# Attention and two expert layers on one core: element steps ahead of low parts, and the opening and operand steps in another order

## The chip, the cores and the metric

The kernel runs on one core of a Trainium2 chip. The metric is the device time in microseconds of the whole program. Engines: PE is TensorE, DVE is VectorE, ACT is ScalarE, POOL is GpSimd, SP is SyncE, which issues the DMAs.

## The reference, cut to what matters

```python
def sm_attn(qq, kk, vv):
    s = scale * np.matmul(qq, kk.transpose(0, 1, 3, 2))
    s = s - np.max(s, axis=-1, keepdims=True)
    a = np.exp(s)
    a = a / (np.sum(a, axis=-1, keepdims=True) + 1e-09)
    return np.matmul(a, vv)
p_packed = sm_attn(p, k, v)                 # 32 packed rows per head
x = sm_attn(q, p_packed, p_packed)          # 8 batches, 8 heads, 576 tokens, 64 wide

xn = x / sqrt(mean(x * x) + 1e-06) * rms_g  # x as 4608 tokens x 512
g = xn @ w_gate                             # 512 x 1536
y = (g * (1.0 / (1.0 + np.exp(-g))) * (xn @ w_val)) @ w_out

h = y @ w_in                                # 512 x 2048
out = (np.maximum(h, 0.0) + alpha * np.minimum(h, 0.0)) @ w_out2
```

All inputs and outputs are float32.

## The kernel before

**Precision.** A product that must be exact to float32 is made of three matmuls in a rounded type (`mm3`, L122 to L124): high by high, high by low, low by high. For each operand ScalarE writes the high part (`split_hi`, L110) and VectorE then subtracts it from the source to give the low part (`split_lo`, L113). In the names h is the high part and l the low one: hh and hl of the activated tile s, in_h and in_l of the output weights, xh and xl of the normed tokens, yh and yl of an operand of the second layer.

**Attention in chains.** `k_steps` makes the packed rows of a batch, `q_steps` (L574 to L697) the tokens of a pair of tiles from them: transposes of q, a product, max (L628), subtraction (L630), Exp on ScalarE, sum and reciprocal (L636 to L638), multiplication (L640), transposition to A2T (L645), a product on TensorE (L656), squares on ScalarE (L680), the factor of the RMS norm (L683, L684 on VectorE, then a power step on GpSimd, L687), its transposition on TensorE (L692) and A2T times factor (L696). A chain stops at each yield; its kind says what may come next: E an element step on VectorE, X one on ScalarE, M and R others, a number a step that needs PSUM banks.

**First layer.** The 4608 tokens go in 12 chunks (0 to 11) of 512 or 320 tokens. In a chunk a loop over 12 slices f of the hidden width does: gate product (`blk_in`), activation s, value product, s times value (L1071), `hsplit` of s into hh and hl, and one slice late the output product (`blk_out(f - 1)`). Between these stand `work(f, at)`, which advances the attention chains of the next chunk (at is the place in the slice, 1 to 4), and `burst`, which issues their TensorE parts; `both` splits the output weights of the next slice. In chunk 0 the even slices use unsplit float32, so only odd slices have low parts.

**Opening.** The gate, value and output weights come as 64-bit words and are narrowed in units, by `narrow`: a first step (L227 on VectorE, L231 on ScalarE) and a second one (L233 on VectorE, L236 on GpSimd). `conv(2)` advances a pair of units by one step. Units 0 to 3 are gv_raw, 4 and 5 are w_raw, then gv_raw again. `wg_job(0, 0)` (L724 and following) multiplies units 0 to 3 by the packed rows of batch 0 in two halves (L733), the first from units 0 and 1, the second from 2 and 3. The lines of the opening from L789 on interleave by hand the chains qa and qb (first and second tile pair of chunk 0) and `conv`. Loads of later units wait until the slots of narrowed ones are free.

**Second layer.** Five pairs of token blocks (twice 512, three times, and twice 384 twice) are multiplied by a scheme of seven products. `prep` (L848 and following) makes the seven operands of a pair, for two halves kk, from y that the first layer stored: differences on VectorE (`less`, L861) and splits. `load_rows(pair, kk)` (L836 to L843) loads y on SP. `prep(0)` runs through the last chunk, `prep(pr + 1)` in the part of pair pr that computes 41 output blocks of the table LATER, in the order b5, c2, b6, d3, a1 (8 blocks each, and one c4): one step at each odd index k_, the rest at the pair's end. Ahead of a c2 block (n == 2) `combine_next` adds a subtraction (L1144) on VectorE.

The order of the instructions on each engine is that of the code: the schedule is manual.

Of the kernel before, what the change touches and what calls it, by code (L numbers as in the profile page):

```python
# [18 lines left out]
def attention_moe_moe2_kernel(ctx, tc, q, k, v, p, w_gate, w_val, w_out, rms_g, w_in2, w_out2, alpha, out):  # L19
# [8 lines left out]
    NF = FF // 128  # L28
# [32 lines left out]
    NP1 = len(CH)  # L61
# [50 lines left out]
    def split_lo(lo, src, hi):  # L112
        nc.vector.tensor_tensor(out=lo, in0=src, in1=hi.bitcast(F32), op=ALU.subtract)  # L113
# [12 lines left out]
    with tc.manual_schedule():  # L126
# [227 lines left out]
        steady, KEPT = [0], 1  # L354
        have, NRO = set(), {"h": 2, "l": 3}

        def both(u):
            h, l = [ring.tile([128, 4, 128], F32R, tag="o" + x, name="in_" + x, bufs=NRO[x]) for x in "hl"]
            split_hi(h, raw[u])
            lf, kept = l.rearrange("p c x -> p (c x)").bitcast(F32), lo_dram[u[1]]  # L360
            if u[1] in have and steady[0] > KEPT:
                nc.sync.dma_start(out=lf, in_=kept)
            elif steady[0]:
                nc.gpsimd.tensor_tensor(out=l, in0=raw[u], in1=h.bitcast(F32), op=ALU.subtract)
            else:
                split_lo(l, raw[u], h)
            if steady[0] == KEPT:
                nc.sync.dma_start(out=kept, in_=lf)
                have.add(u[1])
            in_s[u] = (h, l)  # L370
# [430 lines left out]
        xh, xl = new_x()  # L801
# [6 lines left out]
        some(qb, 6)  # L808
        conv(2)
        warmup(3)  # L810
        some(qa, 4)
        some(qb, 3)
        conv(2)
        warmup(3)
        some(qa, 3)
        x_split(ids_a, xh, xl, o_a)
        some(qb, 4)
        conv(2)
        conv_to(4)
        wg_job(0, 0)  # L820
        some(qb, 3)
        x_split(ids_b, xh, xl, o_b)
        assert qa.kind is None and qb.kind is None
        conv_to(5)

        def hsplit(h, n):
            hh = ring.tile([128, T], F32R, tag="hh", name="hh")[:, 0:n]
            hl = ring.tile([128, T], F32R, tag="hl", name="hl")[:, 0:n]
            split_hi(hh, h)
            split_lo(hl, h, hh)  # L830
            return hh, hl

        OPERANDS = ("b11", "b21", "b22", "t4", "t1", "t2", "t3")
# [97 lines left out]
        for c, (t0, n, cuts) in enumerate(CH):  # L931
# [106 lines left out]
            for f in range(NF):  # L1038
                if c == 0 and f == 1:
                    held, hold[0] = hold[0], None  # L1040
                    for i in held:
                        load_q(i)
                if c == 6 and f == 6:
                    nc.sync.dma_start(out=alpha_sb, in_=alpha.rearrange("(f p) -> p f", p=128))
                if c == 0:
# [2 lines left out]
                if last:  # L1048
                    if f == 0:
                        assert next(late, late) is late  # L1050
                        y_rows.append(load_rows(0, 0))
                        prepare = prep(0)
                    if f > 0:
                        next(prepare, None)
                    if f in (2, 4, 6, 8, 10):
                        next(prepare, None)
                    if f > 2:
                        load_next()
# [12 lines left out]
                nc.vector.tensor_tensor(out=s, in0=s, in1=tv, op=ALU.mult)  # L1071
                for jb in JOBS[c].get(f, ()) if c else ():
                    wg_job(*jb)
                hs[f] = s if c == 0 and f % 2 == 0 else hsplit(s, n)
                work(f, 2)
                burst(f, 2)
                work(f, 3)
                late_step(c, f, True)
# [119 lines left out]
        for pr, (t0, w) in enumerate(PAIRS):  # L1198
# [148 lines left out]
            for k_ in range(2, len(LATER)):  # L1347
                combine_next(k_ + 2)
                if k_ + 1 < len(LATER):
                    next(splits[k_ + 1])  # L1350
                next(splits[k_])
                while len(fill) > LAG:
                    fill.pop(0)()
                if after:
                    one_after()
                elif k_ % 2:
                    next(prepare, None)
            for _ in prepare:
                pass
# [37 lines left out]
```

## Time and profile before

| | |
|---|---|
| runs, us | 1611.49, 1612.0, 1614.06 (median 1612.0) |
| profiled execution, us | 1614.24 |
| its span, first to last instruction, us | 1612.5 |
| TensorE busy | 1564.3 us, 97% of the span |
| VectorE busy | 1156.4 us, 72% |
| ScalarE busy | 886.8 us, 55% |
| GpSimd busy | 174.6 us, 11% |
| mean granted clock of TensorE | 0.988 |

Some 1.7 us of the profiled execution lie outside the span. The stages in its time: opening to 52 us, chunk 0 to 162, chunks 1 to 10 to 845, chunk 11 to 889, then the second layer. Busy time of TensorE includes time in which a matmul of a group waits for the next operand inside it, so short waits are best read from the start times of neighbouring instructions and the "idle before" in brackets, which names what ended the wait.

### The profile page before, as it was taken

The page shows a single profiled execution, that of the slowest core. Times are in us where ns is not written, and L with a number is a line of the kernel's source. Part 1 is how long each engine was busy: PE and PEld are TensorE (multiplying, and loading weights), DVE is VectorE, ACT ScalarE, POOL GpSimd, SP SyncE. Part 2 cuts the span into 40 slices and gives each one's busy share as a digit, 9 for nine tenths or more (in the row PEclk, how much of TensorE's full clock was granted, in tenths as well). Part 3 has the DMA queues.
Part 4 walks back from the last instruction along what each step waited for, and adds up shares of the span by engine and source line. Part 5 has one row for each costly group of instructions (what it writes and reads, how often), then busy time and mean ns, then how long its engine had stood idle before and what let it go on. Part 6 is the DMA issues. An engine that isn't in the chain of part 4 may idle for free.

```text
span 1612.5 us, 31856 instructions
## 1 busy us (share of the span) xinstructions
PE 1564.3 (97%) x11762; PEld 1369.4 (85%) x11762; DVE 1156.4 (72%) x2232; ACT 886.8 (55%) x1894; POOL 174.6 (11%) x178
## 2 busy tenths in 40 slices
PE   7699999999999999999999999999999999999999
PEld 5366887887888988888888889988998899999998
DVE  4776666666666766767666678867877797788785
ACT  4556555555456555655555555554654464565554
POOL 1542230111201111112120000000000000000000
PEclk8799999999999999999999999999999999999999
DMA  9886777756777565785646676767676767788876
GB/s 244 255 262 201 232 237 226 244 163 209 246 234 231 163 226 188 251 265 164 209 145 210 185 213 191 242 203 217 182 248 202 211 188 244 261 263 284 263 244 196
DMA packets 239067, 356.29 MB, mean 221 GB/s; under 512 B 63424, under 2 KB 97216, under 8 KB 238912
## 3 DMA queue, kind: packets, MB, share of 16 engines
q1 hardware_dynamic: 238912, 354.25, 70.5%
q8 instruction: 94, 1.54, 0.4%
q14 instruction: 61, 0.50, 0.1%
HBM read 296.50 MB, written 57.67 MB: 220 GB/s over the span
## 4 chain that ended last, share of the span: by engine, by line
PE 80%; DVE 10%; ACT 5%; DMA 3%; issue 1%; SPq 1%; POOL 0%; DVEq 0%; ACTq 0%
PE ps_g L122 12%; PE ps_g L123 12%; PE ps_g L124 12%; PE ps_y L122 9%; PE ps_y L124 8%; PE ps_y L123 8%; PE ps_wg L733 3%; PE ps_v L122 2%; PE ps_v L123 2%; PE ps_v L124 2%; DVE hl L113 2%; PE ps_y L1031 1%; ACT hh L110 1%; DVE wgl L113 1%; DVE s L1071 1%
## 5 line engine op out<-in xcount | busy, mean ns | idle before, releaser
L122 PE MATMUL ps_g<-yh,w 128*128 128x512 f32 (+1 forms) x560 | 206.4, 369 | 0.0
L123 PE MATMUL ps_g<-yl,w 128*128 128x512 f32 (+1 forms) x560 | 206.3, 368 | 0.0
L124 PE MATMUL ps_g<-yh,w 128*128 128x512 f32 (+1 forms) x560 | 205.7, 367 | 0.0
L122 PE MATMUL ps_y<-hh,in_h 128*128 128x320 f32 (+1 forms) x552 | 195.1, 353 | 2.7 <-ACT hh L110 2.6
L123 PE MATMUL ps_y<-hl,in_h 128*128 128x320 f32 (+1 forms) x552 | 185.5, 336 | 2.3 <-DVE hl L113 2.1
L124 PE MATMUL ps_y<-hh,in_l 128*128 128x320 f32 (+1 forms) x552 | 184.4, 334 | 0.0
L110 ACT ACTIVATE hh<-kept 128x512 fp32r<-128x512 f32 (+1 forms) x200 | 116.4, 587 | 102.2 <-PE ps_g L123 49.2
L124 PE MATMUL ps_y<-w,hl 128*128 128x256 f32 x576 | 164.7, 286 | 3.1 <-DVE hl L113 2.3
L123 PE MATMUL ps_y<-w,hh 128*128 128x256 f32 x576 | 162.7, 283 | 0.0
L122 PE MATMUL ps_y<-w,hh 128*128 128x256 f32 x576 | 162.5, 282 | 0.0
L110 ACT ACTIVATE hh<-s 128x320 fp32r<-128x320 f32 (+1 forms) x138 | 71.9, 521 | 149.8 <-DVE s L1071 149.6
L122 PEld LDWEIGHTS ps_y<-hh,in_h 128*128 128x128 f32 x552 | 103.6, 188 | 49.9 <-issue 38.3
L113 DVE TENSOR_TENSOR hl<-kept,hh 128x512 fp32r<-128x512 f32 (+1 forms) x200 | 123.2, 631 | 16.0 <-ACT hh L110 14.9
L1141 DVE TENSOR_TENSOR tmp<-tmp,ps_g 128x512 f32<-128x512 f32 (+2 forms) x140 | 88.3, 631 | 56.0 <-PE ps_g L124 55.9
L124 PE MATMUL ps_g<-w,hl 128*128 128x256 f32 x432 | 122.4, 283 | 0.0
L122 PE MATMUL ps_g<-w,hh 128*128 128x256 f32 x432 | 122.3, 283 | 0.0
L123 PE MATMUL ps_g<-w,hh 128*128 128x256 f32 x432 | 122.3, 283 | 0.0
L113 DVE TENSOR_TENSOR hl<-s,hh 128x320 fp32r<-128x320 f32 (+1 forms) x138 | 77.8, 564 | 56.7 <-ACT hh L110 56.7
L122 PE MATMUL ps_g<-xh,wgh 128*128 128x256 f32 (+3 forms) x352 | 114.2, 324 | 3.3 <-ACT qT L600 1.8
L124 PEld LDWEIGHTS ps_g<-yh,w 128*128 128x128 f32 x560 | 105.2, 188 | 13.4
L122 PEld LDWEIGHTS ps_g<-yh,w 128*128 128x128 f32 x560 | 105.4, 188 | 11.9
L124 PEld LDWEIGHTS ps_y<-w,hl 128*128 128x128 f32 x576 | 109.9, 191 | 6.3 <-DVE hl L113 5.7
(199 smaller groups left out, 4068.9 us busy)
## 6 DMA issues: line engine op xcount, KB each, us to landing
w<-w_dram SPq DMA_DIRECT2D x280, 256.0 KB, 3.1
w<-o_dram SPq DMA_DIRECT2D x280, 256.0 KB, 3.0
gv_raw<-gv_dram SPq DMA_DIRECT2D x168, 256.0 KB, 4.1
in_l<-lo_dram SPq DMA_DIRECT2D x119, 256.0 KB, 4.5
w<-in_moe_w_out_dram SPq DMA_DIRECT2D x28, 512.0 KB, 5.2
w_dram<-w7o SPq DMA_DIRECT2D x56, 256.0 KB, 2.5
o_dram<-w7o SPq DMA_DIRECT2D x56, 256.0 KB, 2.9
vt<-in_v_dram SPq DMA_DIRECT2D x16, 576.0 KB, 6.2
```

The source lines that it names most:

```text
L110: nc.scalar.activation(out=hi, in_=src, func=ACTF.Copy)
L113: nc.vector.tensor_tensor(out=lo, in0=src, in1=hi.bitcast(F32), op=ALU.subtract)
L122: nc.tensor.matmul(out=o, lhsT=lh, rhs=rh, start=first, stop=False, skip_group_check=more)
L123: nc.tensor.matmul(out=o, lhsT=lh, rhs=rl, start=False, stop=False, skip_group_check=more)
L124: nc.tensor.matmul(out=o, lhsT=ll, rhs=rh, start=False, stop=last, skip_group_check=more)
L733: nc.tensor.matmul(out=ts[g][h * NP:(h + 1) * NP, :], lhsT=ppG[b][e * D:(e + 1) * D, c_, :], rhs=us[c_][e * D:(e + 1) * D, :], start=True, ...
L1031: nc.tensor.matmul(out=ybk[d], lhsT=w[:, d, :], rhs=h, start=f == 0, stop=f == NF - 1)
L1071: nc.vector.tensor_tensor(out=s, in0=s, in1=tv, op=ALU.mult)
L1141: nc.vector.tensor_tensor(out=out, in0=x, in1=y, op=ALU.add)
```

## The change

It moves instructions; their number and kinds stay the same, and TensorE's order too. (A) In the opening the second narrowing step of units 2 and 3 comes ahead of the second tile pair's factor. (B) In chunk 0 the low part of the output weights waits for the next `hsplit`. (C) In chunks 1 to 10, at slices 1 to 9, the chains' steps of place 2 come between hh and hl. (D) The first y rows are loaded in slice 9 of chunk 10 instead of slice 0 of chunk 11. (E) No operand step is issued at an odd index with a c2 block among the next three.

```diff
--- before.py
+++ after.py
@@ -354,6 +354,8 @@
         steady, KEPT = [0], 1
         have, NRO = set(), {"h": 2, "l": 3}
 
+        lo_later = []
+
         def both(u):
             h, l = [ring.tile([128, 4, 128], F32R, tag="o" + x, name="in_" + x, bufs=NRO[x]) for x in "hl"]
             split_hi(h, raw[u])
@@ -363,7 +365,7 @@
             elif steady[0]:
                 nc.gpsimd.tensor_tensor(out=l, in0=raw[u], in1=h.bitcast(F32), op=ALU.subtract)
             else:
-                split_lo(l, raw[u], h)
+                lo_later.append(lambda: split_lo(l, raw[u], h))
             if steady[0] == KEPT:
                 nc.sync.dma_start(out=kept, in_=lf)
                 have.add(u[1])
@@ -808,18 +810,21 @@
         some(qb, 6)
         conv(2)
         warmup(3)
-        some(qa, 4)
+        some(qa, 3)
+        conv(2)
+        some(qa, 1)
+        warmup(3)
+        some(qb, 3)
+        some(qa, 3)
+        conv(2)
+        x_split(ids_a, xh, xl, o_a)
         some(qb, 3)
         conv(2)
-        warmup(3)
-        some(qa, 3)
-        x_split(ids_a, xh, xl, o_a)
-        some(qb, 4)
-        conv(2)
-        conv_to(4)
+        some(qb, 1)
         wg_job(0, 0)
         some(qb, 3)
         x_split(ids_b, xh, xl, o_b)
+        conv(2)
         assert qa.kind is None and qb.kind is None
         conv_to(5)
 
@@ -827,7 +832,8 @@
             hh = ring.tile([128, T], F32R, tag="hh", name="hh")[:, 0:n]
             hl = ring.tile([128, T], F32R, tag="hl", name="hl")[:, 0:n]
             split_hi(hh, h)
-            split_lo(hl, h, hh)
+            while lo_later:
+                lo_later.pop(0)()
             return hh, hl
 
         OPERANDS = ("b11", "b21", "b22", "t4", "t1", "t2", "t3")
@@ -1040,6 +1046,8 @@
                     held, hold[0] = hold[0], None
                     for i in held:
                         load_q(i)
+                if c == NP1 - 2 and f == 9:
+                    y_rows.append(load_rows(0, 0))
                 if c == 6 and f == 6:
                     nc.sync.dma_start(out=alpha_sb, in_=alpha.rearrange("(f p) -> p f", p=128))
                 if c == 0:
@@ -1048,7 +1056,6 @@
                 if last:
                     if f == 0:
                         assert next(late, late) is late
-                        y_rows.append(load_rows(0, 0))
                         prepare = prep(0)
                     if f > 0:
                         next(prepare, None)
@@ -1071,8 +1078,14 @@
                 nc.vector.tensor_tensor(out=s, in0=s, in1=tv, op=ALU.mult)
                 for jb in JOBS[c].get(f, ()) if c else ():
                     wg_job(*jb)
-                hs[f] = s if c == 0 and f % 2 == 0 else hsplit(s, n)
-                work(f, 2)
+                exact = c == 0 and f % 2 == 0
+                hs[f] = s if exact else hsplit(s, n)
+                if c and 0 < f < NF - 2:
+                    work(f, 2)
+                if not exact:
+                    split_lo(hs[f][1], s, hs[f][0])
+                if not (c and 0 < f < NF - 2):
+                    work(f, 2)
                 burst(f, 2)
                 work(f, 3)
                 late_step(c, f, True)
@@ -1353,7 +1366,7 @@
                     fill.pop(0)()
                 if after:
                     one_after()
-                elif k_ % 2:
+                elif k_ % 2 and not any(n == 2 for _, n, _ in LATER[k_ + 1:k_ + 4]):
                     next(prepare, None)
             for _ in prepare:
                 pass
```

Three places in the order of the instructions. The first is the opening; GpSimd there, before and now (w_175, w_178 and w_181 are units 1, 2 and 3; s_128 and s_369 the first and second tile pair's factor):

```order
L236 TENSOR_TENSOR gv_raw<-gv_raw,w_175 128x512
L687 TENSOR_TENSOR s_128<-s_128,mhalf 128x2
L687 TENSOR_TENSOR s_369<-s_369,mhalf 128x2
L236 TENSOR_TENSOR gv_raw<-gv_raw,w_178 128x512
L236 TENSOR_TENSOR gv_raw<-gv_raw,w_181 128x512
L236 TENSOR_TENSOR w_raw<-w_raw,w_184 128x512
L236 TENSOR_TENSOR w_raw<-w_raw,w_186 128x512
```

```order
L236 TENSOR_TENSOR gv_raw<-gv_raw,w_175 128x512
L689 TENSOR_TENSOR s_128<-s_128,mhalf 128x2
L236 TENSOR_TENSOR gv_raw<-gv_raw,w_178 128x512
L236 TENSOR_TENSOR gv_raw<-gv_raw,w_181 128x512
L689 TENSOR_TENSOR s_369<-s_369,mhalf 128x2
L236 TENSOR_TENSOR w_raw<-w_raw,w_184 128x512
L236 TENSOR_TENSOR w_raw<-w_raw,w_186 128x512
```

The two narrowing steps of units 2 and 3 went from behind the power step of the second tile pair to ahead of it.

VectorE there, before and now:

```order
L645 STREAM_TRANSPOSE A2T<-A_426 128x512
L227 TENSOR_SCALAR gv_raw<-w_178 128x512
L227 TENSOR_SCALAR gv_raw<-w_181 128x512
L696 TENSOR_TENSOR A2T<-A2T,ps_at 128x512
L113 TENSOR_TENSOR xl<-A2T,xh 128x2x256
L683 TENSOR_TENSOR s_369<-s_369 128x2
L684 TENSOR_SCALAR s_369<-s_369 128x2
L233 SCALAR_TENSOR_TENSOR gv_raw<-w_178,gv_raw 128x512
L233 SCALAR_TENSOR_TENSOR gv_raw<-w_181,gv_raw 128x512
L227 TENSOR_SCALAR w_raw<-w_184 128x512
```

```order
L647 STREAM_TRANSPOSE A2T<-A_426 128x512
L698 TENSOR_TENSOR A2T<-A2T,ps_at 128x512
L233 SCALAR_TENSOR_TENSOR gv_raw<-w_178,gv_raw 128x512
L233 SCALAR_TENSOR_TENSOR gv_raw<-w_181,gv_raw 128x512
L113 TENSOR_TENSOR xl<-A2T,xh 128x2x256
L227 TENSOR_SCALAR w_raw<-w_184 128x512
L227 TENSOR_SCALAR w_raw<-w_186 128x512
L685 TENSOR_TENSOR s_369<-s_369 128x2
L686 TENSOR_SCALAR s_369<-s_369 128x2
L113 TENSOR_TENSOR wgl<-ps_wg,wgh 128x512 x2
```

The second narrowing step of units 2 and 3 went ahead of xl and of the factor's L683 (now L685); the first step of both w_raw units went ahead of it too.

The second place is VectorE in chunk 9, one slice, before and now (A_9336 and A_9411 are the two tile pairs of chunk 10):

```order
L1071 TENSOR_TENSOR s<-s,ps_v 128x320
L113 TENSOR_TENSOR hl<-s,hh 128x320
L636 TENSOR_REDUCE s_9252<-A_9336 128x16
L637 TENSOR_SCALAR s_9252<-s_9252 128x16
L638 RECIPROCAL s_9252<-s_9252 128x16
L630 TENSOR_TENSOR A_9411<-A_9411,s_9253 128x512
L640 TENSOR_TENSOR A_9336<-A_9336,s_9252 128x512
L113 TENSOR_TENSOR w7o<-w_9301,w7o 128x256 x2
L645 STREAM_TRANSPOSE A2T<-A_9336 128x512
```

```order
L1078 TENSOR_TENSOR s<-s,ps_v 128x320
L638 TENSOR_REDUCE s_9252<-A_9336 128x16
L639 TENSOR_SCALAR s_9252<-s_9252 128x16
L640 RECIPROCAL s_9252<-s_9252 128x16
L632 TENSOR_TENSOR A_9411<-A_9411,s_9253 128x512
L113 TENSOR_TENSOR hl<-s,hh 128x320
L642 TENSOR_TENSOR A_9336<-A_9336,s_9252 128x512
L113 TENSOR_TENSOR w7o<-w_9301,w7o 128x256 x2
L647 STREAM_TRANSPOSE A2T<-A_9336 128x512
```

The low part hl went from right behind s to behind four steps of the two chains.

The third is VectorE at the end of pair 0, before and now:

```order
L113 TENSOR_TENSOR hl<-kept,hh 128x512
L113 TENSOR_TENSOR hl<-kept_12306,hh 128x512
L113 TENSOR_TENSOR yl<-y_raw,yh 128x512
L113 TENSOR_TENSOR hl<-kept_12306,hh 128x512
L113 TENSOR_TENSOR yl<-y_raw,yh 128x512
L1141 TENSOR_TENSOR tmp<-tmp,ps_g 128x512 x2
L1141 TENSOR_TENSOR kept<-tmp,ps_g 128x512
```

```order
L113 TENSOR_TENSOR hl<-kept_12306,hh 128x512
L867 TENSOR_TENSOR y_d<-y_raw,y_d 128x512
L113 TENSOR_TENSOR yl<-y_d,yh 128x512
L113 TENSOR_TENSOR hl<-kept_12306,hh 128x512
L867 TENSOR_TENSOR y_d<-y_raw,y_d 128x512
L113 TENSOR_TENSOR yl<-y_d,yh 128x512
L867 TENSOR_TENSOR y_d<-y_raw 128x512
L113 TENSOR_TENSOR yl<-y_d,yh 128x512 x2
L113 TENSOR_TENSOR yl<-y_raw,yh 128x512 x2
L1154 TENSOR_TENSOR tmp<-tmp,ps_g 128x512 x2
L1154 TENSOR_TENSOR kept<-tmp,ps_g 128x512
```

Between the last hl of the pair and the first addition of the next one stand seven instructions of operand steps, where there was one yl.

## Rows read from the trace of the kernel before

**Rows 1.** The page, engines: busy us (share of the span) xinstructions.

```profile
PE 1564.3 (97%) x11762; PEld 1369.4 (85%) x11762; DVE 1156.4 (72%) x2232; ACT 886.8 (55%) x1894; POOL 174.6 (11%) x178
```

**Rows 2.** Windows by stage; columns in the first line; PEclk is the granted clock.

```profile
core 0: us, PE busy (x) PEld busy (x) DVE busy (x) ACT busy (x) POOL busy (x), PEclk, DMA share, GB/s
41.00:52.00 11.00, 6.11 (x24) 1.03 (x20) 4.44 (x9) 3.96 (x13) 3.76 (x3) 0.50 0.66 223
```

**Rows 3.** Timeline of TensorE, opening: start us, us, line op out<-in, [idle before <-releaser].

```profile
46.47 3.16 PE L733 MATMUL ps_wg<-gv_raw,ppG 64*32 64x512 f32 x8 [3.14 <-POOL gv_raw L236]
49.55 0.69 PE L692 MATMUL ps_y<-ident,s 128*128 128x128 f32 x2
52.30 1.22 PE L1021 MATMUL ps_g<-xh,wgh 128*128 128x512 f32 x2 [2.06 <-ACT xh L110]
```

**Rows 4.** Timeline of GpSimd (POOL), opening.

```profile
43.89 1.00 POOL L687 TENSOR_TENSOR s<-s,mhalf 128x2 f32<-128x2 f32 x1 [6.35 <-ACT w L231]
44.86 2.79 POOL L236 TENSOR_TENSOR gv_raw<-gv_raw,w 128x512 int32<-128x512 int32 x2
```

**Rows 5.** Timeline of VectorE (DVE), opening.

```profile
39.17 0.72 DVE L227 TENSOR_SCALAR gv_raw<-w 128x512 int32<-128x512 int32 x2
39.80 0.68 DVE L696 TENSOR_TENSOR A2T<-A2T,ps_at 128x512 f32<-128x512 f32 x1
...
43.65 1.29 DVE L233 SCALAR_TENSOR_TENSOR gv_raw<-w,gv_raw 128x512 int32<-128x512 int32 x2
...
54.43 2.99 DVE L227 TENSOR_SCALAR gv_raw<-w 128x512 int32<-128x512 int32 x2
```

**Rows 6.** Waits of TensorE from 52 to 162 us: total us, times, longest.

```profile
PE ps_at L598 <- DVE s L1071: 1.1, 1, 1.1
PE ps_at L479 <- DVE s L1071: 0.8, 1, 0.8
```

**Rows 7.** Timeline of VectorE, chunk 0.

```profile
103.44 0.69 DVE L113 TENSOR_TENSOR in_l<-w_raw,in_h 128x512 fp32r<-128x512 f32 x1 [0.74 <-ACT in_h L110]
...
105.30 0.69 DVE L1071 TENSOR_TENSOR s<-s,ps_v 128x512 f32<-128x512 f32 x1
```

**Rows 8.** Timeline of VectorE, chunk 9.

```profile
729.80 0.49 DVE L113 TENSOR_TENSOR hl<-s,hh 128x320 fp32r<-128x320 f32 x1 [0.54 <-ACT hh L110]
```

**Rows 9.** Timeline of TensorE, chunk 9.

```profile
731.52 0.31 PE L123 MATMUL ps_y<-hl,in_h 128*128 128x320 f32 x1
...
733.88 0.38 PE L656 MATMUL ps_at<-ppbd,A2T 64*128 64x128 f32 x2 [0.58 <-DVE A2T L645]
```

**Rows 10.** Waits of TensorE from 162 to 845 us: total us, times, longest.

```profile
PE ps_y L123 <- DVE hl L113: 2.1, 7, 0.4
...
PE ps_at L656 <- DVE A2T L645: 1.8, 2, 1.2
PE ps_g L122 <- DVE A L626: 1.0, 1, 1.0
```

**Rows 11.** Timelines of SP's queue and VectorE, start of chunk 11.

```profile
847.02 1.67 SPq L841 DMA_DIRECT2D y_raw<-y_dram  x2
...
852.51 0.69 DVE L861 TENSOR_TENSOR tmp<-y_raw 128x512 f32<-128x512 f32 x1 [3.12 <-DMA y_raw<-y_dram]
```

**Rows 12.** Timeline of TensorE, start of chunk 11.

```profile
855.41 0.42 PE L122 MATMUL ps_y<-hh,in_h 128*128 128x320 f32 x1 [2.32 <-ACT hh L110]
```

**Rows 13.** Windows over the c2 products of pairs 0 to 3, columns as in rows 2.

```profile
1003.69:1016.59 12.90, 12.41 (x99) 11.73 (x97) 12.73 (x22) 6.51 (x11) 0.00 (x0) 1.00 0.70 221
1162.56:1175.45 12.89, 12.41 (x98) 11.71 (x97) 12.72 (x22) 6.50 (x11) 0.00 (x0) 1.00 0.70 222
1321.42:1333.12 11.70, 11.70 (x98) 11.57 (x97) 11.49 (x20) 6.20 (x11) 0.00 (x0) 1.00 0.78 217
1452.76:1462.88 10.12, 9.52 (x74) 8.83 (x73) 9.97 (x22) 5.44 (x12) 0.00 (x0) 1.00 0.75 227
```

**Rows 14.** Timeline of VectorE, end of pair 0 and start of pair 1.

```profile
1047.27 0.68 DVE L113 TENSOR_TENSOR hl<-kept,hh 128x512 fp32r<-128x512 f32 x1
1047.87 0.69 DVE L113 TENSOR_TENSOR yl<-y_raw,yh 128x512 fp32r<-128x512 f32 x1
1051.28 0.69 DVE L1141 TENSOR_TENSOR tmp<-tmp,ps_g 128x512 f32<-128x512 f32 x1 [2.73 <-PE ps_g L124]
```

## The prediction

> **What bounds the kernel now.** I read the engine table of the page first. TensorE is busy 97% of the span [rows 1], so an edit that only moves work of other engines can gain no more than TensorE's waits: the time in which it stands still, and the time that a late operand adds to a group of matmuls. The opening is where such waits are long: between 41 and 52 us TensorE is busy 6.11 of 11.00 us at a granted clock of 0.50, the 1.2 GHz level [rows 2]. After that they are short and scattered, and the question for each part of the change is which of them it reaches. I went through the stages in the order of time: the opening by the timelines of TensorE, GpSimd and VectorE [rows 3 to 5], the MoE chunks by the table of waits and two timelines [rows 6 to 10], the first prepared operands by the transfer they wait for [rows 11, 12], and the second MoE by windows over one group of products of each pair [rows 13, 14]. The profiled execution took 1614.24 us, 2.24 above the median of 1612.0; I sum against it and take the same sum off the median.
>
> **A, the opening.** TensorE does the second half of the first weight job at 46.47 after 3.14 us of idling, put down to GpSimd's gv_raw; it ends at 49.63, since the last gv_raw is ready at 44.86 + 2.79 = 47.65 [rows 3, 4]. Only then comes the transpose of the second tile's factor (49.55), and 2.75 us after it the first product of chunk 0 (52.30). GpSimd had that factor ready at 44.89 [rows 4]. So narrowing of units 2 and 3 is what is late, not the tile. It is late because VectorE issues its L233 pair at 43.65, behind L683 of the second tile, and GpSimd stands behind its own power step at 43.89 [rows 4, 5]. The change puts the L233 pair right behind L696 (39.80) and the GpSimd pair ahead of the power step. L696 itself can start 0.7 earlier, since the L227 pair (39.17, 0.72 us) now stands far ahead of it [rows 5]. Step by step: L696 39.2 to 39.8, L233 pair 1.29 us to 41.1, the GpSimd pair from the first of them on, 40.5 to 43.3; with each engine holding the other up once, 44.4. The power step then ends between 44.9 and 45.4, its transpose follows at 45.0 to 46.0 instead of 49.55, and with the same 2.75 us the first product starts at 47.8 to 48.8. That is 3.5 to 4.5 us; I take **-3.5**, the low end, since what comes next is limited by the same narrowing steps. Those steps move up too: the slots of units 2 and 3 come free some 4 us earlier, and the loads that wait for them with them. Bounds: -6 (the shorter VectorE queue also shortens chunk 0's first block) and 0 (the next narrowing eats it all).
>
> One row speaks against this part. VectorE's L227 pair took 0.72 us at 39.17, but 2.99 us at 54.43, where GpSimd was narrowing [rows 5]. The change puts such a pair, and the L683 of the second tile behind it, just where GpSimd now narrows units 2 and 3. If the pair there takes 2.99 instead of 0.72, the factor is 2.27 us later and the gain falls from 3.5 to 1.2. I count that as a rival. The Trainium skill, page "SBUF — State Buffer", section "SBUF: two separate sides", says that VectorE and GpSimd share one port pair as an exclusive lock, held for a whole instruction by whichever starts first. By that rule the long pair at 54.43 is a lock wait and the same would happen at the new place; the trace agrees as far as 2.99 against 0.72 goes.
>
> **B, low parts of the output weights in chunk 0.** An in_l now stands ahead of s: at 103.44 VectorE first waits 0.74 us for in_h, works 0.69, and s follows at 105.30 [rows 7]. TensorE waits for that s: L598 1.1 us and L479 0.8 us in chunk 0 [rows 6]. Moved behind s and hh, the in_l fills the gap in which VectorE waits for hh anyway. Of the 1.9 us I take **-1.7**; bounds -3 (six places) and 0.
>
> **C, element steps ahead of hl in chunks 1 to 10.** VectorE idles 0.54 us ahead of hl, waiting for hh [rows 8], and so ahead of nearly every hl of those chunks. The chain's element steps now fill that. What is gained is only where TensorE waits for the chain: for A2T 1.8 us in 2 places, one of them 0.58 at 733.88 [rows 9], and for a transposed A 1.0 us in 1 place [rows 10]. Each can give up to the 0.54 by which VectorE is now earlier. What it costs is a later hl. Ahead of the hl at 729.80 now stand 0.68 + 0.17 + 0.25 + 0.63 us of steps (reduction, two small ones, a subtraction); hl would end at about 731.4 instead of 730.29, and TensorE reads it at 731.52 [rows 9]. So there is cover, by a hair at this place and more at most others. I take **-1.3**; bounds -3 and +2 (waits for hl, now 2.1 us in 7 places [rows 10], about double).
>
> **D, first y rows.** SP issues the load at 847.02, behind chunk 10's stores; VectorE starts the first subtraction at 852.51 after 3.12 us of waiting for it [rows 11]. Everything behind it on VectorE, s and hl of the next block included, is late by that, and TensorE waits 2.32 us for hh at 855.41 [rows 12], then loses about 1.2 more in the blocks behind. The load is now issued two iterations and a tail of chunk 10 earlier, far more than the 5.5 us from its issue to the subtraction, so it has landed when it is wanted. The loss goes to the extent of 3.12 us: **-3.1**. On SP it now stands between in_l loads; its slots were last read by narrowing steps in the first half of chunk 10, so it should not hold those loads up, and if it did, TensorE would show a wait for in_l. Bounds -3.7 and -2.
>
> **E, operand steps kept out of the c2 stage.** The 96 products of that stage take 12.90 and 12.89 us in pairs 0 and 1, 11.70 in pair 2, and the 72 of pair 3 take 10.12 where 0.75 x 11.70 = 8.78 would do [rows 13]. VectorE is busy 12.73 of 12.90 there: it has an extra subtraction per block, and the operand steps on top. Excess: 1.20 + 1.19 + 0 + 1.34 = 3.7 us, which goes when five steps per pair leave. They don't vanish: seven VectorE instructions instead of one now stand between the last hl of a pair (1047.27) and the first addition of the next (1051.28), where there were 2.73 us of idling [rows 14]. Six more, at the 0.60 us from start to start [rows 14], make 3.6, so that addition is some 0.9 late, and the fourth product waits for it. I take 0.5 for each of four boundaries, 2.0 (bounds 0 and 3.6). Net **-1.7**; bounds -3.7 and 0.
>
> **Sum.** -3.5 - 1.7 - 1.3 - 3.1 - 1.7 = -11.3: 1602.9 beside the profiled 1614.24, and **1600.7** beside the median.
>
> **The rivals.**
> 1. *The opening gives little*: GpSimd and VectorE hold each other up (above), or chunk 0's narrowing is the bound whatever the first product does. Then A gives 1.2 and B half: -1.2 - 0.85 - 1.3 - 3.1 - 1.7 = -8.2, 1603.8. For it: the 2.99 at 54.43. Against it: the pair stands behind work that ends at 43.3, and the power step would still precede 49.55 by far.
> 2. *Only the transfer is worth anything*: A, B and C are taken up by waits for the next narrowing, and the burst costs what the c2 stage gave. Then D alone, 1608.9, within 0.2% of before (3.2 us, about what a measurement of this kernel can tell from no change).
> 3. *Slower: the low part comes too late.* At some 44 places hl stands behind up to 1.7 us of steps, less the 0.54 of waiting: up to 1.2 late. If the cover of 1.2 us at 731.52 were used up at most places by what shifts along with it, a wait of 0.6 at each would cost 26 us, and the time would be 1612 - 10 + 26 = 1628. It decides from about 17 such places on. Against it: one wait for hl of 0.3 on average in 7 places is all that the chunks show now, so most hl have cover.
> 4. *The burst at a pair's end starves the next pair by more than an addition* (operands of its second half come late as well): 2 us more at each of four, 1608.7.
>
> **Chances.** Forecast 0.58, rival 1 0.24, rivals 2 and 4 0.13 together, rival 3 0.05. Faster by over 0.2%: forecast, rival 1 and a little of the others, 0.86; within 0.2%: 0.10; slower: 0.04. The range takes A at -6 and E at -3.7 on the low side, 1600.7 - 2.5 - 2.0 = 1596, and somewhat less for C at its bound, 1594.5; on the high side it reaches rivals 2 and 4, 1609.
>
> **What would show it.** Right: first product of chunk 0 near 48.3 instead of 52.30; no wait of VectorE for y_raw at the start of the last chunk, and no 2.3 us wait for hh there; the c2 windows near 11.70 (8.78 in pair 3); first addition of a pair about 0.9 late. Wrong: more than 5 us in all of waits for hl between 162 and 845; an L227 or L683 stretched beyond 2 us around 42; TensorE waiting for an operand at a pair's start; or the first product early and the clock or a later narrowing wait in chunk 0 giving it back by 160 us.

## The result, and the profile after

| | before | the change |
|---|---|---|
| median, us | 1612.62 (4 runs, 1611.49 to 1614.06) | 1597.72 (4 runs, 1597.44 to 1600.92) |
| ratio | | 0.9912, 95% interval 0.9895 to 0.9929 |
| profiled execution, us | 1614.24 | 1597.45 |
| its span, us | 1612.5 | 1595.7 |
| mean granted clock | 0.988 | 0.995 |

The kernel is faster by 14.9 us. 1600.7 was predicted, with 1594.5 to 1609.0 as the range, so the forecast held, and the gain was 3.6 us larger than the 11.3 forecast. Lines of the changed file are 2 to 13 higher than those of before: L687 is L689, L696 is L698, L861 is L867, L1071 is L1078, L1141 is L1154.

TensorE runs the same 11762 matmuls in the same order in every kernel here. So the same matmul can be looked up in two timelines, and the difference of its start times shows how much was won up to it. Six of them cut the program into stages; the numbers are starts in us, then the lengths between them. The marks are the transposition of the first tile pair's factor (L692, L694 now), the first product of chunk 0, of chunk 1, of chunk 11, of the second layer, and the start of the last matmul.

| kernel | profiled us | factor at | to chunk 0 | chunk 0 | chunks 1-10 | chunk 11 | second layer |
|---|---|---|---|---|---|---|---|
| before | 1614.24 | 37.60 | 14.70 | 110.36 | 683.07 | 43.02 | 719.43 |
| the change | 1597.45 | 34.51 | 10.04 | 107.90 | 680.83 | 39.80 | 718.35 |
| difference | 16.79 | 3.09 | 4.66 | 2.46 | 2.24 | 3.22 | 1.08 |

The last six differences make 16.75. Not all of it is the change's. A product with q that no moved instruction precedes starts 3.62 us earlier already, before and now:

```profile
29.25 0.76 PE L615 MATMUL ps_y<-qT,ppB 64*32 64x256 f32 x16 [0.86 <-ACT qT L600]
```

```profile
25.63 0.76 PE L617 MATMUL ps_y<-qT,ppB 64*32 64x256 f32 x16 [2.08 <-ACT qT L602]
```

That part belongs to the start of the execution (see e1 and the last section); the other 13.1 us lie behind moved instructions and are taken as the change's, though chunk 0 and chunks 1 to 10 also vary from execution to execution (see the experiments). At the factor only 3.09 of the 3.62 are left. The factor comes 8.35 us behind that product before and 8.36 in e1, which has the opening of before, but 8.87 or 8.88 in all ten profiles with the new opening. So part A costs 0.52 us ahead of the factor, and of the 4.66 behind it 4.14 are a gain.

**Opening (A).** TensorE's timeline of the changed kernel, which answers to [rows 3]:

```profile
40.82 1.05 PE L735 MATMUL ps_wg<-gv_raw,ppG 64*32 64x512 f32 x4 [0.23 <-POOL gv_raw L236]
42.55 0.43 PE L694 MATMUL ps_y<-ident,s 128*128 128x128 f32 x2 [0.68 <-POOL s L689]
44.54 0.73 PE L1027 MATMUL ps_g<-xh,wgh 128*128 128x512 f32 x2 [1.56 <-ACT xh L110]
```

GpSimd and VectorE there, which answer to [rows 4, 5]:

```profile
37.46 3.31 POOL L236 TENSOR_TENSOR gv_raw<-gv_raw,w 128x512 int32<-128x512 int32 x2 [3.01 <-ACT xh L110]
41.80 0.69 POOL L689 TENSOR_TENSOR s<-s,mhalf 128x2 f32<-128x2 f32 x1 [1.04 <-DMA w<-in_moe_w_val_dram]
```

```profile
36.65 1.28 DVE L233 SCALAR_TENSOR_TENSOR gv_raw<-w,gv_raw 128x512 int32<-128x512 int32 x2
37.85 1.77 DVE L113 TENSOR_TENSOR xl<-A2T,xh 128x512 fp32r<-128x512 f32 x1
39.54 1.84 DVE L227 TENSOR_SCALAR w_raw<-w 128x512 int32<-128x512 int32 x2
```

The second half of the first weight job waits 0.23 us for GpSimd instead of 3.14, and the factor of the second tile pair follows it after a wait of 0.68. Beside GpSimd's pair (37.46 to 40.77) VectorE's xl took 1.77 us and its L227 pair 1.84, where 0.69 and 0.72 were seen without it: the two do hold each other up, by 2.2 us in all, and the power step starts at 41.80, not right at 40.77.

The 0.52 us that A costs come from the same effect, at a place that the order of the instructions shown ahead of the prediction leaves out. The first narrowing step of units 2 and 3 stood behind the first factor (39.17, 0.72 us long). Now it stands ahead of it, beside GpSimd's narrowing of units 0 and 1 (30.01 to 33.05). VectorE there, now and before:

```profile
30.39 2.94 DVE L227 TENSOR_SCALAR gv_raw<-w 128x512 int32<-128x512 int32 x2
33.25 0.15 DVE L685 TENSOR_TENSOR s<-s 128x2 f32<-128x2 f32 x1
```

```profile
35.36 1.12 DVE L683 TENSOR_TENSOR s<-s 128x2 f32<-128x2 f32 x1 [1.28 <-ACT ps_at L680]
```

The pair takes 2.94 us, and L685 starts 1.41 us behind the last of the squares on ScalarE that it needs (31.84). Before, L683 started right behind them and took 1.12 us itself, beside GpSimd; so the loss is less than the 1.41.

**Chunk 11 (D).** SP's queue and VectorE, which answer to [rows 11]: the y rows are issued at 809.22, 24 us ahead of the chunk, and the first subtraction has no wait ahead of it.

```profile
809.22 0.90 SPq L847 DMA_DIRECT2D y_raw<-y_dram  x2
```

```profile
836.85 0.68 DVE L867 TENSOR_TENSOR tmp<-y_raw 128x512 f32<-128x512 f32 x1
```

**Second layer (E).** Windows over the c2 products of pairs 0 to 3, which answer to [rows 13], and the waits of TensorE in the whole layer:

```profile
988.00:999.52 11.52, 11.52 (x99) 11.52 (x98) 9.86 (x17) 5.58 (x9) 0.00 (x0) 1.00 0.69 185
1146.39:1157.91 11.52, 11.52 (x99) 11.52 (x97) 9.85 (x17) 5.58 (x9) 0.00 (x0) 1.00 0.61 187
1304.78:1316.30 11.52, 11.52 (x98) 11.52 (x97) 9.72 (x17) 5.47 (x9) 0.00 (x0) 1.00 0.65 181
1436.38:1445.02 8.64, 8.64 (x74) 8.64 (x73) 7.78 (x18) 4.62 (x9) 0.00 (x0) 1.00 0.80 246
```

```profile
PE ps_g L122 <- DVE tmp L1154: 2.2, 4, 0.8
PE ps_y L124 <- DVE hl L113: 1.2, 2, 0.6
```

The products now take 11.52 us three times and 8.64, in all 43.20 where they took 47.61: 4.4 less. New is the first line of the waits: four times, 2.2 us of idling in all, TensorE waits for the first addition of a pair. By the start times around them the four places cost 0.90, 0.90, 0.54 and 1.04 us, 3.4 in all, so the layer gains only 1.1.

### The profile page after: what moved, and what is told of

Same layout as the page of the kernel before. It is cut to its first block, busy times and chain, and to the rows that moved or that the text cites. A ratio compares the mean times of both kernels' runs of the same rounds, so it can differ in the third digit from the quotient of the medians.

```text
span 1595.7 us, 31864 instructions
## 1 busy us (share of the span) xinstructions
PE 1555.4 (97%) x11762; PEld 1364.9 (86%) x11762; DVE 1161.2 (73%) x2232; ACT 887.8 (56%) x1894; POOL 175.7 (11%) x178
## 4 chain that ended last, share of the span: by engine, by line
PE 82%; DVE 8%; ACT 5%; DMA 2%; issue 1%; SPq 1%; POOL 0%; DVEq 0%; ACTq 0%; POOLq 0%
PE ps_g L122 13%; PE ps_g L123 12%; PE ps_g L124 12%; PE ps_y L122 9%; PE ps_y L123 9%; PE ps_y L124 9%; PE ps_wg L735 3%; PE ps_v L122 3%; PE ps_v L123 2%; PE ps_v L124 2%; PE ps_y L1037 1%; DVE hl L113 1%; ACT hh L110 1%; DVE wgl L113 1%; PE ps_at L658 1%
## 5 line engine op out<-in xcount | busy, mean ns | idle before, releaser
L1154 DVE TENSOR_TENSOR tmp<-tmp,ps_g 128x512 f32<-128x512 f32 (+2 forms) x140 | 88.4, 631 | 45.8 <-PE ps_g L124 45.8
L123 PEld LDWEIGHTS ps_g<-yl,w 128*128 128x128 f32 x560 | 105.5, 188 | 11.3
L1074 DVE SCALAR_TENSOR_TENSOR s<-s,ps_g 128x320 f32<-128x320 f32 (+1 forms) x132 | 70.6, 535 | 59.4 <-ACT s L1069 58.6
```

Source lines behind the costliest of these rows:

```text
L123: nc.tensor.matmul(out=o, lhsT=lh, rhs=rl, start=False, stop=False, skip_group_check=more)
L1074: nc.vector.scalar_tensor_tensor(out=s, in0=s, scalar=1.0, in1=tg, op0=ALU.add, op1=ALU.mult)
L1154: nc.vector.tensor_tensor(out=out, in0=x, in1=y, op=ALU.add)
```

## The experiments

Each is one edit of the changed kernel (e9 of e7), timed beside the kernel before. Their stages:

| kernel | median us | profiled us | factor at | to chunk 0 | chunk 0 | chunks 1-10 | chunk 11 | second layer |
|---|---|---|---|---|---|---|---|---|
| e1 opening as before | 1603.16 | 1606.10 | 37.43 | **14.70** | 109.30 | 680.47 | 39.81 | 718.35 |
| e2 y load as before | 1601.86 | 1601.56 | 34.93 | 10.04 | 107.89 | 681.03 | **43.14** | 718.49 |
| e3 low part first | 1601.30 | 1600.46 | 34.81 | 10.04 | 108.79 | **682.64** | 39.80 | 718.35 |
| e4 operand steps as before | 1600.19 | 1599.34 | 34.92 | 10.04 | 107.78 | 681.31 | 39.82 | **719.46** |
| e5 the change again | 1597.60 | 1601.16 | 36.52 | 10.54 | 108.84 | 681.07 | 39.78 | 718.38 |
| e6 in_l at once | 1602.20 | 1601.96 | 36.44 | 10.04 | **109.79** | 681.31 | 39.79 | 718.55 |
| e7 owed steps spread | 1595.49 | 1594.63 | 34.91 | 10.04 | 108.34 | 680.57 | 39.80 | **714.95** |
| e8 w_raw behind factor | 1599.72 | 1598.12 | 34.25 | **10.71** | 108.00 | 680.95 | 39.80 | 718.37 |
| e9 v before q, on e7 | 1596.35 | 1595.53 | 33.94 | **10.89** | 109.82 | 680.06 | 39.79 | 714.99 |
| e10 e7 again | 1596.45 | 1598.19 | 37.26 | 10.04 | 107.54 | 682.57 | 39.79 | 714.95 |

Chunk 11 and the second layer repeat to 0.2 us, the way from the factor to chunk 0 mostly to 0.01. Chunk 0 and chunks 1 to 10 vary by up to 2.3 and 2.5 us between kernels that are the same there, and the time of the factor by 3.7. Medians are rougher still for parts of this size: undone one by one, the five parts raise them by 5.4, 4.1, 3.6, 2.5 and 4.5 us, 20 in all, where the whole change took 14.9 off; all five are taken against the one median of the change, whose error so counts five times. So verdicts rest on the stages, in the two that vary on the waits of the same matmul in all twelve profiles, and a median only rules out what is 3 us away.

### e1: the opening as before

```diff
-        some(qa, 3)
-        conv(2)
-        some(qa, 1)
-        warmup(3)
-        some(qb, 3)
-        some(qa, 3)
-        conv(2)
-        x_split(ids_a, xh, xl, o_a)
+        some(qa, 4)
         some(qb, 3)
         conv(2)
-        some(qb, 1)
+        warmup(3)
+        some(qa, 3)
+        x_split(ids_a, xh, xl, o_a)
+        some(qb, 4)
+        conv(2)
+        conv_to(4)
         wg_job(0, 0)
         some(qb, 3)
         x_split(ids_b, xh, xl, o_b)
-        conv(2)
```

> The changed kernel with the opening of before. Theory: the opening part is worth about 4.7 us up to the first product of chunk 0 and about 5.5 by 66 us, all of it between the transposition of the first tile pair's factor and that product: that distance, 10.0 us in the changed kernel and 14.7 before, goes back to 14.7, and the median to about 1603. The other 3.1 us by which the two profiled executions differ at 34 us belong to the granted clock of the first 30 us and not to the change, so the factor's transposition may come anywhere from 34.5 to 37.6. Rival: the whole 7.8 us by which the first product came earlier is the opening's; then the transposition is at 37.6 again, the first product near 52.3 and the median near 1605.5.

The way from the factor to chunk 0 is back at 14.70, to the hundredth, and the factor is 8.36 us behind the product with q instead of 8.87 or 8.88. So A is worth 4.14 us up to the first product. Behind it, the stretch up to the weight job's second wait for gv_raw (at 57.51 in the change) takes 13.32 us here and 12.97 to 12.99 in the nine profiles with A and B: another 0.3. Chunk 0 as a whole is about 1 us longer than the middle of the others, but most of that arises at 121 us, at a weight job where e9, with the new opening, loses as much. The factor came at 37.43 in this profile, as the rival has it. But its times, 1602.13 to 1606.10 with a median 5.4 above the change's, fit 5.5 better than 7.8, and e5, e6 and e10 have the new opening and the factor at 36.4 to 37.3. So the rival falls, and the start is taken to be a matter of the execution. One thing speaks for the rival: the two profiles with the old opening are the latest at the product with q (29.25 and 29.07; 25.37 to 28.38 in the nine others that load q first). Against it: nothing was moved ahead of that product, and the profiled execution of e1 was 2.3 to 4.0 us longer than its three others.

### e2: the y load as before

```diff
-                if c == NP1 - 2 and f == 9:
-                    y_rows.append(load_rows(0, 0))
...
                         assert next(late, late) is late
+                        y_rows.append(load_rows(0, 0))
```

> The changed kernel with the first y rows loaded in slice 0 of chunk 11 again. Theory: VectorE waits about 3.1 us for y_raw again, TensorE some 2.3 us for hh in that chunk, and the median is 3.3 us higher, about 1601. Rival: with the other parts in, VectorE has room there and less than 1.5 us come back, about 1599.

VectorE's timeline of this run, at the start of chunk 11:

```profile
837.05 0.49 DVE L113 TENSOR_TENSOR hl<-s,hh 128x320 fp32r<-128x320 f32 x1 [0.54 <-ACT hh L110]
840.76 0.69 DVE L867 TENSOR_TENSOR tmp<-y_raw 128x512 f32<-128x512 f32 x1 [3.22 <-DMA y_raw<-y_dram]
```

The wait is back with 3.22 us, TensorE's longest wait for hh in that chunk is 2.4 us, and chunk 11 takes 43.14 instead of 39.80, 3.3 more, as the theory has it. The other parts gave VectorE no room there.

### e3: the low part first

```diff
-                if c and 0 < f < NF - 2:
-                    work(f, 2)
                 if not exact:
                     split_lo(hs[f][1], s, hs[f][0])
-                if not (c and 0 < f < NF - 2):
-                    work(f, 2)
+                work(f, 2)
```

> The changed kernel with hl ahead of the element steps of place 2 again, in chunks 1 to 10. Theory: the 0.54 us gap ahead of hl is back in these slices, TensorE's waits for the chains come back and waits for hl get shorter; between 162 and 845 us the program is 2.3 us slower, the median about 1600. Rival: the gain there is not from the order of the two but from what the chunk begins with; then the distance over chunks 1 to 10 stays within 0.7 us of the changed kernel's, 1598.

Waits of TensorE over chunks 1 to 10, of the change and of this run:

```profile
PE ps_y L123 <- DVE hl L113: 2.4, 7, 0.7
...
PE ps_wg L735 <- ACT E L462: 1.6, 3, 1.1
PE ps_at L658 <- DVE A2T L647: 1.1, 1, 1.1
PE ps_g L122 <- DVE A L628: 0.7, 3, 0.4
```

```profile
PE ps_wg L735 <- ACT E L462: 2.1, 4, 1.2
PE ps_y L123 <- DVE hl L113: 2.1, 7, 0.3
...
PE ps_at L658 <- DVE A2T L647: 1.8, 2, 1.2
PE ps_g L122 <- DVE A L628: 1.3, 3, 1.0
```

The stage takes 682.64, 1.8 more than the change and 1.3 more than the longest of e1, e2 and e4 to e8; e10, the same there as the change, has 682.57 once, so the stage alone does not prove it. The waits do: those for the chain (E, A2T, A) are 3.4 us with the late low part and 5.2 with the early one, a difference of 1.8, and the wait for hl is 2.4 against 2.1. They can be followed matmul by matmul: five waits of 0.23 to 0.58 us for the chain stand in the kernel before and in this one and in none of the ten profiles with the late low part, and three more are longer in both. So C's worth of about 1.8 does not hang on the varying length of the stage. In the change, chain steps stand ahead of hl in 37 places; the late low part costs 0.3 us in all.

### e4: the operand steps as before

```diff
-                elif k_ % 2 and not any(n == 2 for _, n, _ in LATER[k_ + 1:k_ + 4]):
+                elif k_ % 2:
```

> The changed kernel with an operand step at every odd index again. Theory: the c2 windows of pairs 0, 1 and 3 take about 1.2, 1.2 and 1.3 us more again, and the four starts of a pair lose their wait of 0.4 to 0.75 us for the first addition: net 1.2 us slower, about 1599. Rival: the four boundary waits cost as much as the c2 waits gave, and the time stays at 1597.7 within 0.4.

The second layer takes 719.46, 1.1 more, as before the change (719.43). The theory's net holds, but both of its terms were too small: the c2 products take 47.59 us again, 4.4 more where 3.7 were expected, and the four waits that go gave back 3.4 (see e7).

### e5: the change again

No edit.

> The changed kernel once more, for a time on the same chip as the three beside it and a second profile. Theory: median within 1.5 us of 1597.7; the stretch up to 34 us may differ by up to 3 us with the granted clock between 12 and 30 us, and nothing else by more than 1 us. Rival: the chip of the first four experiments is slower by 1 to 2 us in every stage, and this reads 1599 with a profile that is longer everywhere.

The median, 1597.60, agrees with the first. The profiled execution was one of the slower (1601.16): 2.01 us of its 3.71 are there at the factor, 0.5 on the way to chunk 0, 0.9 in chunk 0. Each of the last two is within the theory's 1 us, together they are 1.4; the other stages agree to 0.3.

### e6: in_l at once

```diff
-                lo_later.append(lambda: split_lo(l, raw[u], h))
+                split_lo(l, raw[u], h)
```

> The changed kernel with in_l of chunk 0 subtracted at once, ahead of s, as before. Theory: TensorE's waits for s at odd slices come back, about 1 us at 96 and 0.5 at 114 us; 1.4 us over chunk 0, median 1.4 above the changed kernel's. Rival: chunk 0 is bound by the narrowing steps on VectorE and GpSimd in any order, and less than 0.5 us comes back.

Waits of TensorE in chunk 0, of this run and of the change:

```profile
PE ps_wg L735 <- POOL gv_raw L236: 2.2, 2, 1.2
PE ps_at L600 <- DVE s L1078: 1.1, 1, 1.1
PE ps_at L481 <- DVE s L1078: 0.8, 1, 0.8
```

```profile
PE ps_wg L735 <- POOL gv_raw L236: 1.6, 2, 1.2
...
PE ps_at L600 <- DVE s L1078: 0.8, 1, 0.8
```

Chunk 0 takes 109.79, against 107.54 to 108.84 in the others with both A and B but e9. As e9 has 109.82, the stage alone does not prove it. The waits do. Three of them are longer in the two kernels without B, the one before and this one, than in the ten profiles with it: at L481 0.84 and 0.76 us against none, at L600 1.05 twice against 0.25 to 0.77, and the weight job's second wait for gv_raw (the second of the two at L735) 0.98 and 0.97 against 0.37 or 0.38. In the last, in_l had stood between the second narrowing steps of two units on VectorE (in this run at 56.16, between 55.56 and 56.76), and GpSimd waits for those. By the start times around them the three are 0.6, 1.0 and 0.3 us, so B is worth about 1.9; 1.4 was expected.

### e7: the owed steps spread

```diff
+            owed = 0
...
-                elif k_ % 2 and not any(n == 2 for _, n, _ in LATER[k_ + 1:k_ + 4]):
+                elif k_ % 2:
+                    if any(n == 2 for _, n, _ in LATER[k_ + 1:k_ + 4]):
+                        owed += 1
+                    else:
+                        next(prepare, None)
+                elif owed and k_ > 16:
                     next(prepare, None)
+                    owed -= 1
```

> The changed kernel, with the operand steps that it keeps out of the c2 stage issued one by one at even indices from 18 on, right behind that stage, so that one yl and not six steps more stands at the end of a pair. Theory: the wait for the first addition of a pair (0.41 to 0.75 us at four places, 2.2 in all) goes, the c2 windows stay at 11.7 us, and the median is 2.2 us below the changed kernel's, the fastest yet. Rival: VectorE is full there too, at 1.4 us a block, and low parts come late behind the c2 stage by as much as the boundary gains.

Waits of TensorE in the second layer of this run, and VectorE at the end of pair 0 in it and in the change:

```profile
PE ps_y L124 <- DVE hl L113: 1.2, 2, 0.6
```

```profile
1031.43 0.69 DVE L113 TENSOR_TENSOR yl<-y_raw,yh 128x512 fp32r<-128x512 f32 x1
1034.79 0.69 DVE L1154 TENSOR_TENSOR tmp<-tmp,ps_g 128x512 f32<-128x512 f32 x1 [2.67 <-PE ps_g L124]
```

```profile
1030.19 0.68 DVE L113 TENSOR_TENSOR hl<-kept,hh 128x512 fp32r<-128x512 f32 x1
...
1034.11 1.28 DVE L113 TENSOR_TENSOR yl<-y_raw,yh 128x512 fp32r<-128x512 f32 x2
1035.32 0.68 DVE L1154 TENSOR_TENSOR tmp<-tmp,ps_g 128x512 f32<-128x512 f32 x1
```

The addition waits for TensorE again (2.67 us of idling) and not TensorE for it; in the change VectorE is busy without a gap from the last hl to the addition. The layer is 3.4 us shorter than in the change, 714.95, and e10 has the same. This is the fastest kernel of the study: 1595.49 beside 1597.60 for the change on the same chip, ratio to before 0.9894 (0.9879 to 0.9909). It also gives E's terms: the four boundaries cost 3.4 us in the change, and the gain of 4.5 against before is nearly all the c2 stage's, whose products take 43.20 us here as in the change.

### e8: w_raw behind the factor

```diff
-        some(qb, 3)
-        conv(2)
-        some(qb, 1)
+        some(qb, 4)
         wg_job(0, 0)
+        conv(2)
```

> The changed kernel with the first narrowing step of the two w_raw units behind the first weight job's splits instead of ahead of the second tile pair's factor. Theory: the L227 pair, 1.84 us long beside GpSimd there, no longer holds the factor up; the power step starts at about 40.8 instead of 41.8 and the first product of chunk 0 comes 0.7 to 1.0 us earlier; but the pair is only moved to where narrowing is the bound, so by 70 us at most 0.3 is left, or it is up to 0.5 slower. Rival: what the first product gains stays, and the end is 0.7 us or more earlier.

GpSimd, VectorE and TensorE of this run:

```profile
40.88 0.70 POOL L689 TENSOR_TENSOR s<-s,mhalf 128x2 f32<-128x2 f32 x1 [0.36 <-DVE s L686]
```

```profile
42.29 0.69 DVE L113 TENSOR_TENSOR wgl<-ps_wg,wgh 128x512 fp32r<-128x512 f32 x1 [0.97 <-ACT wgh L110]
42.90 0.75 DVE L227 TENSOR_SCALAR w_raw<-w 128x512 int32<-128x512 int32 x2
43.57 0.68 DVE L698 TENSOR_TENSOR A2T<-A2T,ps_y 128x512 f32<-128x512 f32 x1
```

```profile
44.96 0.73 PE L1026 MATMUL ps_g<-xh,wgh 128*128 128x512 f32 x2 [2.90 <-ACT xh L110]
```

The power step starts at 40.88, 0.66 us earlier than in the change when both are counted from the first factor, and the L227 pair takes 0.75 instead of 1.84 where GpSimd is idle. But it now stands between the last split of the weight job (42.29) and L698 (43.57), and the first product comes 0.67 later after the factor, not earlier. Both expectations of an earlier product are missed; that nothing is won in the end holds. What the pair lost beside GpSimd in the change, 1.1 us, ran beside the weight job, and so cost little: the job's last split on VectorE ends 8.73 us behind the first factor in both kernels.

### e9 and e10: v before q, and e7 again

```diff
+        load_kv()
         for i in range(2):
             load_q(i)
-        load_kv()
```

> The kernel with the owed steps spread, and the first half of v loaded ahead of the first two q tiles. Theory: the up to 3 us by which executions of one kernel differ before 34 us come from the moment v lands: where TensorE's first product with v starts after about 15.5 us, the engine has idled longer and its granted clock is at the 1.2 GHz level somewhere between 12 and 30 us. With v earlier that product starts before 14.3 us in every profile and the low level falls later and for less time; the median is 1 to 2 us below that of the same kernel without it. Rival: q then lands later, the products with q wait instead, and the time is the same or up to 1 us longer.

> The kernel with the owed steps spread once more, beside the one with v first. Theory: median within 1 us of 1595.5; its profile agrees with the earlier one from 34 us on within 1 us once the difference of the first 34 us is taken off.

Windows on the opening: e9's, and e10's:

```profile
18.00:24.00 6.00, 4.29 (x37) 2.46 (x34) 4.34 (x13) 2.45 (x8) 0.00 (x0) 1.00 1.02 343
...
36.00:42.00 6.00, 6.00 (x32) 2.08 (x31) 5.74 (x9) 4.05 (x12) 4.01 (x3) 0.50 1.07 277
```

```profile
18.00:24.00 6.00, 5.48 (x73) 3.94 (x72) 1.83 (x8) 2.07 (x6) 0.00 (x0) 0.60 0.97 299
```

With v loaded first, the first product with v starts at 12.79 instead of 15.11, the clock is 1.00, the 2.4 GHz level, from 18 to 24 us instead of 0.60, and the factor comes at 33.94, the earliest of all. Then the clock is at the low level all through 36 to 42, and the way to chunk 0 takes 10.89 instead of 10.04. Chunk 0 takes 2.3 more than in e10, of which some 1.0 arise at a weight job at 114 us, far behind that stretch. The medians are equal (1596.35 and 1596.45). The theory's first half holds, its gain does not come: the low level came later, with other work under it. That the low level took the whole gain is not shown, since chunk 0 lost more than the way to it. e10's median is as expected; its chunks 1 to 10 are 2.0 us longer than e7's, more than the 1 us expected. Two matmuls make that up, with 1.5 us at 374 us (a wait of 1.13 us for s) and 0.6 at 646 us (0.54 for hh); in e7 neither waits. Why this execution has these waits stays open.

## Why the prediction was right, and where it was off

- **A, -3.5 forecast, -4.1 to the first product and -0.3 behind it.** The chain behind the first factor was as worked out. Taken back by the 3.62 us that this execution was ahead, the GpSimd pair ended at 44.39 (43.3 to 44.4 forecast), the second factor's transposition was at 46.17 (45.0 to 46.0) and the first product at 48.16 (47.8 to 48.8). One step failed: L696 was to start 0.7 us earlier because the L227 pair stands far ahead of it, as if the pair cost nothing there. The pair took 2.94 us, held the first factor up by 0.52, and L696 came only 0.1 earlier (39.70 against 39.80, taken back). The whole term was undersized all the same, because I took the low end, on the ground that the next narrowing would take part of it back; e1 shows that nothing was taken back.
- **The rival on the port (rival 1).** The instructions did stretch beside GpSimd: the L227 pair of units 2 and 3 to 2.94 us, xl by 1.1 us and the next L227 pair by 1.1. That agrees in kind with the rule of the Trainium skill, page "SBUF — State Buffer", section "SBUF: two separate sides"; e8 shows the pair at 0.75 where GpSimd is idle. So the rival's 2.99 came nearly to the hundredth, but on the first factor and not on the second, and its price was wrong: 2.27 us were assumed on the chain. At the first factor 0.52 came of it. At the second, the squares on ScalarE (to 40.26) and the weight job (its last split on VectorE ends at 43.24) covered most, and moving the pair away won nothing.
- **B, -1.7 forecast, about -1.9 measured** (e6), but not at the places forecast alone. The wait at L479 went whole. The one at L598 fell from 1.05 to 0.77 only. The rest, 0.6, is the weight job's wait for gv_raw, which the prediction did not have: that the sum came out is in part luck.
- **C, -1.3 forecast, about -1.8** (e3, by the waits). The cover for hl was there: the wait for hl rose by 0.3 us in all, where the bound had allowed 2. Of the two A2T waits one went, 0.58 at 733.88, as the 0.54 gap said; the other is still 1.07 at 727.48 in the changed kernel, since VectorE waits for ScalarE's w7o there. The wait for a transposed A fell from 1.04 to 0.44, and four waits of 0.2 to 0.5 us that the sum did not name went too.
- **D, -3.1 forecast, -3.2 measured**, and -3.3 when undone (e2).
- **E, -1.7 forecast, -1.1 measured**, from terms that were both too small: the c2 stage gave 4.4, not 3.7, since its undisturbed length is 11.52 and not the 11.70 of pair 2, which had itself lost a little; and a boundary cost 0.8 us, not 0.5. The direction, the place and the waiting instruction were right.
- **Slower (rival 3)** would have needed waits for hl of 10 us; 2.4 were seen, with 37 places instead of the 44 assumed. Rival 2 fell with A, B and C, and rival 4 since TensorE waits at a pair's start for the first addition alone and for no operand.
- **What the prediction passed over.** Behind the opening the waits were said to be short and scattered. One is not: in chunk 0 TensorE idles 4.48 us for one s, in the kernel before at 71.74, and 4.47 or 4.48 in the eleven other profiles. No part of the change reaches it. VectorE comes to that s behind narrowing steps, among them an L227 pair of 2.92 us beside GpSimd, where such a pair took 0.72 at 39.17. Whether another order there would win it was not tried.

```profile
PE ps_at L440 <- DVE s L1071: 4.5, 1, 4.5
```

```profile
67.57 2.92 DVE L227 TENSOR_SCALAR gv_raw<-w 128x512 int32<-128x512 int32 x2
```

The parts sum to 13.1 in the profiles against 11.3. The medians differ by 14.9, with an interval of some 2.7 us to either side; the remaining 1.8 are within what the start of an execution varies by, and I can't attribute them further.

## What to carry to other kernels

Where one engine is 97% busy, find the waits of that engine by stage and ask of each edit which of them it reaches; five small edits then add up nearly as worked out. Work that is kept out of a crowded stage must be given a place, or it piles up at the next boundary: spread over the stage behind, the same rule gave 4.5 us in the second layer instead of 1.1. Where the order of the work is the same on the bound engine, compare the start of the same instruction in two profiles: in stages that repeat to 0.2 us it separates 1 us parts that medians with a spread of 3 us can't, and in a stage that varies, the waits of the same matmul over all profiles do. Put the first mark ahead of everything that was moved: the factor here was behind a moved instruction, and hid 0.5 us of loss.

## What the runs showed that was not expected

The factor of the first tile pair comes anywhere between 33.9 and 37.6 us, 36.5 against 34.5 in two executions of the changed kernel, and TensorE's granted clock differs along with it. Windows of the profile before and after the change, in the stretch where no moved instruction lies, with TensorE's first product with v:

```profile
18.00:24.00 6.00, 5.37 (x66) 4.01 (x70) 2.04 (x9) 1.91 (x6) 0.00 (x0) 0.50 0.77 248
```

```profile
18.00:24.00 6.00, 4.85 (x42) 3.03 (x40) 4.31 (x13) 2.08 (x7) 0.00 (x0) 1.00 1.04 383
```

```profile
15.76 0.88 PE L488 MATMUL ps_y<-vt,E1T 96*32 96x64 f32 x48 [1.56 <-DMA vt<-in_v_dram]
```

```profile
14.15 0.88 PE L490 MATMUL ps_y<-vt,E1T 96*32 96x64 f32 x48 [0.73 <-DMA vt<-in_v_dram]
```

Where v landed late, the engine idled 1.56 us instead of 0.73 and then ran from 18 to 24 us at 0.50, the 1.2 GHz level, while it was granted full clock there in the other profile; in e10 it was 0.60. But e7 had its first product with v at 15.18 and full clock there, so the landing of v alone does not settle it. e9 shows that an earlier v moves the low stretch and does not remove it. What else sets when it falls was not tried.
